# Holding GpSimd's work until the VectorE op ahead of the planner's last two-port VectorE op has ended

## The chip, the cores and the metric

The kernel runs on one NeuronCore of one Trainium2 chip. The metric is device time in microseconds (us), from the first to the last instruction of one execution, with medians over several executions. Every execution counted here is classed "fast" unless I say otherwise; where the granted clock of TensorE (PE) was below 1.0 in an execution, I say so too, since with one core the class alone does not show it.

## The reference

One pre-norm transformer layer on x of 2048 x 512 in bfloat16: attention with 32 heads of 16, then a gated feed-forward part of width 1792.

```python
h  = x + softmax(q @ k.T * 16**-0.5) @ v @ wo        # q, k, v from layernorm(x) @ wqkv, 32 heads
h2 = h + (gelu(ln(h) @ w_gate) * (ln(h) @ w_up)) @ w_down
```

The costly part is the exponential of 32 x 2048 x 2048 scores: the exponentials on ScalarE alone keep it busy for 724.1 of the 812.7 us of the profiled execution of before.

## The kernel before

The kernel holds a planner. It describes all work as operations with an engine, an estimated length, tiles that are read and written, and priorities; it plays them through on its own clock, and whenever an operation is started there, it is emitted into the instruction stream of its engine. The chip then runs these fixed streams. Besides its place in the stream and the conflict that `port` stands for (below), what holds an instruction back on the chip are semaphores, and these come from the data: a read waits for the write, a write for earlier reads.

```python
class Op:
    def __init__(self, eng, dur, fns, reads=(), writes=(), ..., port=False, ...):
        ...
        self.port = port or eng == "pool"

class Sched:
    def _ready(self, op):                    # earliest planned start
        ...
        return max([self.done[t] + LATS.get((t[0], op.eng), LAT) + lag for t in toks ...]
                   + [self.port if op.port else 0.0])

    def _emit(self, op, start):
        ...
        extra = op.extra() if op.extra else ()
        for tok in extra:
            start = max(start, self.done[tok] + LATS.get((tok[0], op.eng), LAT))
        ...
        end = start + op.dur
        if op.port:
            self.port = end
        # ... cut: transfers, PE groups
        for i, fn in enumerate(op.fns):
            tok = P.op(op.eng, fn, reads=op.reads, writes=op.writes, sig=(i == n - 1), extra_deps=extra)
```

`port` stands in the plan for a conflict between VectorE and GpSimd. All GpSimd ops ("pool") and some VectorE ops ("dve") take it, and in the plan they take it one after the other. A VectorE op with `port=True` is called two-port below, the products included; "two-port", "port" and "queue" are names for what the rows of the trace show, and no more is claimed. In 44 rows, 20.7 us in all, a two-port VectorE op takes longer than usual, 1.79 us in place of 0.94 for instance (L1730 at 458.56 us, shown in the prediction). Each of the 44 overlaps a GpSimd op that began earlier and ends 0.54 to 0.55 us (L1728, L1735) or 0.80 to 0.82 us (L1730) after it. Where no GpSimd row overlaps, no row of these lines is longer than 0.70, 0.70 and 0.96 us. The other way round, the GpSimd product L1732 takes 1.15 us in 88 rows and about 1.53 in 35; these 35 begin while a two-port VectorE op runs and end 1.01 to 1.02 us after it. So the one that came first holds the other up. VectorE's L1715, which reads PSUM and is not two-port, shows nothing of the kind: 54 of its 492 rows lie wholly under a GpSimd row, and none is longer than 0.69 us. The chip does not keep the order of the plan: 43 of the 44 are blocked by a GpSimd op that was emitted after them.

Exponentials are made in two ways. ScalarE takes most (778 instructions, L1347). For the rest, in groups of four tiles, VectorE makes an exponential from bit patterns (the `pbank` tiles lie in PSUM, where PE's products land; the `dXE` tiles lie in SBUF; lines are shortened here, cuts are marked by dots):

```python
    def dconv(G, j, b):      # four times for each group, from PSUM, not marked `port` (L1715)
        yield Op("dve", 0.603, lambda e: e.tensor_scalar(out=dXE[...][:, 0, j, :], in0=pbank[:, b, :], ...), ...)

    def dchain(G):           # n = 4 tiles of 512, nd = 3 of them for VectorE
        yield Op("dve", 0.07 + 0.133 * n, lambda e: e.tensor_scalar(out=W, in0=X, ...), ..., port=True)          # L1728
        yield Op("dve", 0.066 + 0.267 * nd, lambda e: e.tensor_tensor(out=W[:, 0:nd, :], ..., op=ALU.mult),
                 ..., port=True)                                                                                  # L1730
        for j in range(nd, n):
            yield Op("pool", TPOOL, lambda e, j=j: e.tensor_tensor(out=W[:, j, :], ..., op=ALU.mult),
                     reads=[kW[j], kX[j], kW[0]], writes=[kW[j]], port=True)                                      # L1732
        yield Op("dve", ..., lambda e, ...: e.tensor_scalar(out=X, in0=X, ...), reads=kX + kW, ..., port=True)    # L1735
        sch.add(group_pv(G), -5.1)     # PE multiplies both halves with V
```

There are 123 such groups. GpSimd also masks Q (L1533), scales attention outputs (L1841) and makes the layer norm's statistics (L1426, L1428, L1910, L1911).

## Time and profile before

| | before |
|---|---|
| median | 814.82 us (814.54 to 814.97, 3 runs) |
| busy: PE, ScalarE, VectorE, GpSimd | 97%, 95%, 93%, 30% |
| chain that ended last | PE 49%, VectorE 30%, ScalarE 10% |

In the profile's rows "L1730 DVE ..." is line 1730 of the kernel on VectorE, then output and input tiles, the count, the busy time in us and the mean of one in ns, and after the bar the idle time ahead of these instructions with what ended most of it. A row of waits reads: who, for whom, us in total, times, longest. A row of the timeline reads: start, length, engine, line, what, and in brackets an idle time before it. The rows of before stand in the prediction.

### The profile page before, as it was taken

To read this page: it belongs to the slowest core of one execution; us is meant where nothing else is said; L and a number is where in the kernel's file an instruction comes from. 1 tells how busy PE (TensorE), PEld (TensorE's weight loads), DVE (VectorE), ACT (ScalarE), POOL (GpSimd) and SP (SyncE) were. 2 spreads that over 40 slices of the span, in tenths; PEclk is the share of its full clock that TensorE was granted. 3 is DMA by queue.
4 is the path that set the end of the run, shared out by engine and by line. 5 is a ranking of instruction groups with operands and counts; after the bars stand their busy time and mean duration, and the time that the engine had idled before them with its cause. 6 is when DMAs were issued, how large, how long until landed. Compare 5 with 4: busy or idle time off the path is not lost.

```text
span 812.7 us, 20343 instructions
## 1 busy us (share of the span) xinstructions
PE 792.2 (97%) x8342; PEld 276.0 (34%) x8342; DVE 758.9 (93%) x1236; ACT 769.8 (95%) x815; POOL 246.6 (30%) x283
## 2 busy tenths in 40 slices
PE   8999999999999999999999999999999999999998
PEld 4222222222222222222233333333443343444557
DVE  8679999999999999999999999999999999999965
ACT  5899999999999999999999999999999999999972
POOL 3513345532343222122143232223224222233210
PEclk9999999999999999999999999999999999999999
DMA  6200000610021000010011000010001100110000
GB/s 208 52 8 1 7 8 7 252 48 8 7 53 28 8 7 1 8 28 21 23 46 30 11 9 21 14 28 27 8 21 28 27 8 8 28 29 16 15 22 19
DMA packets 50022, 24.33 MB, mean 30 GB/s; under 512 B 39296, under 2 KB 48896, under 8 KB 49920
## 3 DMA queue, kind: packets, MB, share of 16 engines
q1 hardware_dynamic: 49776, 22.88, 10.8%
q8 instruction: 67, 1.10, 0.5%
q14 instruction: 35, 0.29, 0.1%
q10 hardware_dynamic: 144, 0.07, 0.0%
HBM read 11.80 MB, written 2.10 MB: 17 GB/s over the span
## 4 chain that ended last, share of the span: by engine, by line
PE 49%; DVE 30%; ACT 10%; issue 5%; POOL 2%; DMA 0%; DVEq 0%; ACTq 0%; POOLq 0%
PE pbank L1341 31%; PE pbank L1340 14%; DVE dXE L1715 12%; ACT PT L1347 8%; DVE dXE L1730 5%; DVE dXE L1728 4%; PE pbank L2090 4%; DVE dXE L1735 4%; DVE GUT L1981 1%; POOL dXE L1732 1%; ACT GUT L1994 1%; DVE OA L1819 1%; DMA xnT<-xn_sb 0%; ACT L1347 0%; POOL xn_sb L1442 0%
## 5 line engine op out<-in xcount | busy, mean ns | idle before, releaser
L1347 ACT ACTIVATE PT<-pbank 128x1024 bf16<-128x1024 f32 x778 | 724.1, 1080 | 13.4 <-PE pbank L1341 10.2
L1341 PE MATMUL pbank<-QT,KT 32*128 32x512 bf16 (+1 forms) x2304 | 346.9, 359 | 8.4 <-DVE dXE L1715 3.3
L1715 DVE TENSOR_SCALAR dXE<-pbank 128x512 uint16<-128x512 f32 x492 | 323.0, 680 | 8.8 <-PE pbank L1341 6.7
L1732 POOL TENSOR_TENSOR dXE<-dXE 128x512 f16<-128x512 f16 x123 | 155.3, 1263 | 369.2 <-DVE dXE L1730 369.2
L1341 PEld LDWEIGHTS pbank<-QT,KT 32*128 32x128 bf16 x2304 | 89.2, 91 | 294.3 <-ACT PT L1347 201.9
L1341 PE MATMUL pbank<-PT,VA 128*32 128x256 bf16 (+2 forms) x2708 | 130.1, 292 | 0.0
L1730 DVE TENSOR_TENSOR dXE<-dXE 128x1536 f16<-128x1536 f16 x123 | 122.1, 993 | 1.1
L1728 DVE TENSOR_SCALAR dXE<-dXE 128x2048 uint16<-128x2048 uint16 x123 | 94.3, 767 | 0.1
L1735 DVE TENSOR_SCALAR dXE<-dXE 128x2048 uint16<-128x2048 uint16 x123 | 88.1, 720 | 5.8 <-POOL dXE L1732 4.8
L1341 PE MATMUL pbank<-dXE,VA 128*32 128x256 f16 (+2 forms) x1752 | 76.2, 289 | 2.0 <-DVE dXE L1735 1.9
L1340 PE MATMUL pbank<-hnT_c,wg_sb 128*128 128x256 bf16 (+2 forms) x392 | 70.4, 291 | 0.0
L1341 PEld LDWEIGHTS pbank<-PT,VA 128*32 128x32 bf16 x2708 | 47.4, 96 | 60.3 <-issue 57.1
L2090 PE MATMUL pbank<-ones_bf,zero_bf 128*128 128x512 bf16 x201 | 66.0, 386 | 0.0
L1340 PE MATMUL pbank<-hnT_c,wu_sb 128*128 128x256 bf16 (+2 forms) x392 | 58.0, 289 | 3.9 <-DVE GUT L2009 3.2
L1340 PE MATMUL pbank<-wd_sb,GUT 128*128 128x512 bf16 (+1 forms) x238 | 59.9, 369 | 0.0
L1841 POOL TENSOR_TENSOR Otok<-OAT,LINV 128x128 bf16<-128x128 bf16 (+2 forms) x52 | 30.1, 593 | 80.5 <-DVE LINV L1835 79.9
L1341 PEld LDWEIGHTS pbank<-dXE,VA 128*32 128x32 bf16 x1752 | 31.0, 96 | 32.2 <-issue 17.2
L1340 PE MATMUL pbank<-xnT,wqkv_sb 128*128 128x512 bf16 (+1 forms) x152 | 38.2, 349 | 0.9 <-DMA xnT<-xn_sb 0.8
L2009 DVE TENSOR_TENSOR GUT<-pbank,GUT 128x512 bf16<-128x512 f32 (+1 forms) x57 | 36.6, 670 | 1.9 <-PE pbank L1340 1.3
L1340 PEld LDWEIGHTS pbank<-hnT_c,wu_sb 128*128 128x128 bf16 x392 | 29.7, 98 | 24.1 <-issue 9.1
L1981 DVE CAST GUT<-pbank 128x512 bf16<-128x512 f32 (+1 forms) x53 | 35.4, 672 | 1.4 <-PE pbank L1340 1.3
L1533 POOL TENSOR_SCALAR QT<-QT,qmask 128x512 bf16<-128x512 bf16 x30 | 26.3, 883 | 32.7 <-DVE QT L1530 31.8
(82 smaller groups left out, 344.1 us busy)
## 6 DMA issues: line engine op xcount, KB each, us to landing
xres<-in_A_x_dram SPq DMA_DIRECT2D x16, 128.0 KB, 2.2
out_dram<-out_sb SPq DMA_DIRECT2D x15, 128.0 KB, 1.7
wg_sb<-in_B_w_gate_dram SPq DMA_DIRECT2D x1, 1792.0 KB, 7.1
wu_sb<-in_B_w_up_dram SPq DMA_DIRECT2D x1, 1792.0 KB, 11.1
wd_sb<-in_B_w_down_dram SPq DMA_DIRECT2D x1, 1792.0 KB, 15.3
x_sb<-in_A_x_dram SPq DMA_DIRECT2D x3, 512.0 KB, 9.2
wqkv_sb<-in_A_wqkv_dram SPq DMA_DIRECT2D x1, 896.0 KB, 8.5
x_sb<-in_A_x_dram SPq DMA_DIRECT2D x2, 256.0 KB, 2.9
```

What stands on the lines that cost most here:

```text
L1340: return lambda e: e.matmul(o, l, r, start=start, stop=stop)
L1341: return lambda e: e.matmul(o, l, r, start=start, stop=stop, tile_position=tile)
L1347: return lambda e: e.activation(out=o, in_=i, func=func, **kw)
L1715: yield Op("dve", 0.603, lambda e: e.tensor_scalar(out=dXE[G["k"] % NX][:, 0, j, :], in0=pbank[:, b, :], scalar1=XMIN + 1024.0 * CENTER, s ...
L1728: yield Op("dve", 0.07 + 0.133 * n, lambda e: e.tensor_scalar(out=W, in0=X, scalar1=0x3ff, scalar2=0xb800, op0=ALU.bitwise_and, op1=ALU.bi ...
L1730: yield Op("dve", 0.066 + 0.267 * nd, lambda e: e.tensor_tensor(out=W[:, 0:nd, :].bitcast(F16), in0=W[:, 0:nd, :].bitcast(F16), in1=X[:, 0 ...
L1732: yield Op("pool", TPOOL, lambda e, j=j: e.tensor_tensor(out=W[:, j, :].bitcast(F16), in0=W[:, j, :].bitcast(F16), in1=X[:, j, :].bitcast( ...
L1735: yield Op("dve", 0.07 + 0.133 * (h1 - h0), lambda e, h0=h0, h1=h1: e.tensor_scalar(out=X[:, h0:h1, :], in0=X[:, h0:h1, :], scalar1=0x7c00 ...
L1841: yield Op("pool" if turned else "dve", 0.15 + 0.55 / len(slots) if turned else 0.06 + 0.28 / len(slots), lambda e, o4=o4, lx=lx, o_ap=o_a ...
L1981: yield Op("dve", 0.07 + 0.001042 * n * CHUNKS[c], lambda e: e.tensor_copy(out=o_ap, in_=i_ap), reads=[("pb", b)], writes=keys, extra=dE)
L2009: yield Op("dve", 0.07 + 0.001042 * n * CHUNKS[c], lambda e: e.tensor_tensor(out=o_ap, in0=u_ap, in1=o_ap, op=ALU.mult), reads=[("pb", b)] ...
L2090: return Op("pe", TMM, lambda e: e.matmul(pbank[:, b, :], zero_bf[:], ones_bf[:], start=False, stop=False, skip_group_check=True), reads=[ ...
```

## The change

The intent is to make the chip follow the plan where VectorE and GpSimd hold each other up. Let X be the last two-port VectorE op emitted before a GpSimd op. Each GpSimd op now depends, besides on its data, on the VectorE op that stands just ahead of X. So GpSimd is meant not to take the port ahead of X, and yet to stand ready when X ends. Where the new wait ends later than the waits that were there, I call the GpSimd op held.

```diff
         self.port = 0.0
+        self.port_tok = self.dve_tok = None
@@ _emit
         extra = op.extra() if op.extra else ()
+        if op.eng == "pool" and self.port_tok:
+            extra = list(extra) + [self.port_tok]
@@ after the instruction is placed
+            if op.eng == "dve":
+                if op.port:
+                    self.port_tok = self.dve_tok
+                self.dve_tok = tok
```

## The prediction

20.3 - 8, about 12 us, x 0.55 is 6.6 us, two thirds of it were taken as 4.5, and 814.8 - 4.5 is 810.3 us. "Lock", here and in the expectations, is what I call the port.

> **What bounds the kernel now.** I read the page first, then the waits, then the chain of work that ended last, then the timeline of VectorE and GpSimd side by side. There is one core at full clock throughout, so no state and no die is in question. The totals by stretch (columns: stretch, its length, then busy time and instruction count of PE, weight loads, VectorE, ScalarE, GpSimd, then clock, DMA share, GB/s) show three engines that are full at once:
>
> ```profile
> 40.00:780.00 740.00, 726.63 (x7624) 240.25 (x7623) 714.72 (x1125) 730.22 (x768) 226.41 (x235) 1.00 0.10 25
> ```
>
> In these 740 us ScalarE lacks 9.8 us, PE 13.4 us, VectorE 25.3 us. VectorE's work can become shorter by any amount; as long as the 778 exponentials stay on ScalarE, the steady stage cannot give back much more than what ScalarE and PE lose there. The waits say what they lose:
>
> ```profile
> ACT PT L1347 <- PE pbank L1341: 10.2, 21, 1.7
> PE pbank L1341 <- DVE dXE L1715: 3.3, 9, 0.7
> PE pbank L1341 <- DVE dXE L1735: 1.9, 6, 0.7
> DVE dXE L1735 <- POOL dXE L1732: 4.8, 6, 1.3
> ```
>
> ScalarE waits for score products of PE (10.2 us in 21 waits), and PE in turn for VectorE. The chain puts VectorE on 30% of the span. Now the three VectorE lines of the "other exponential" chain (mask, product, mask) and GpSimd's fourth of that product, in the page's groups:
>
> ```profile
> L1732 POOL TENSOR_TENSOR dXE<-dXE 128x512 f16<-128x512 f16 x123 | 155.3, 1263 | 369.2 <-DVE dXE L1730 369.2
> L1730 DVE TENSOR_TENSOR dXE<-dXE 128x1536 f16<-128x1536 f16 x123 | 122.1, 993 | 1.1
> L1728 DVE TENSOR_SCALAR dXE<-dXE 128x2048 uint16<-128x2048 uint16 x123 | 94.3, 767 | 0.1
> L1735 DVE TENSOR_SCALAR dXE<-dXE 128x2048 uint16<-128x2048 uint16 x123 | 88.1, 720 | 5.8 <-POOL dXE L1732 4.8
> ```
>
> L1728 and L1735 are the same operation on the same size, yet they average 767 and 720 ns. The timeline shows why: nearly all take 0.68 us, and a few much more. One case, VectorE's rows first, then GpSimd's:
>
> ```profile
> 456.98 0.95 DVE L1730 TENSOR_TENSOR dXE<-dXE 128x1536 f16<-128x1536 f16 x1
> 457.84 0.69 DVE L1728 TENSOR_SCALAR dXE<-dXE 128x2048 uint16<-128x2048 uint16 x1
> 458.56 1.79 DVE L1730 TENSOR_TENSOR dXE<-dXE 128x1536 f16<-128x1536 f16 x1
> 460.27 0.68 DVE L1715 TENSOR_SCALAR dXE<-pbank 128x512 uint16<-128x512 f32 x1
> ```
>
> ```profile
> 458.00 1.54 POOL L1732 TENSOR_TENSOR dXE<-dXE 128x512 f16<-128x512 f16 x1 [6.43 <-DVE dXE L1730]
> ```
>
> ```profile
> 461.01 0.60 PE L1341 MATMUL pbank<-QT,KT 32*128 32x512 bf16 x3 [0.70 <-DVE dXE L1715]
> ```
>
> GpSimd is released 0.07 us after the first L1730 ends, loses to L1728, which has just begun, and takes 1.54 us in place of 1.15. Then the second L1730 loses to GpSimd: 1.79 us in place of 0.94, that is 0.85 us blocked, until 459.54 when GpSimd ends. PE then stands still for 0.70 us and ScalarE for 0.61 us.
>
> [...] of 492 L1715 (from PSUM), 480 last 650 to 699 ns and none longer, with GpSimd busy or not. [...] here L1732 falls cleanly into 88 of 1.15 us and 35 of about 1.53, so I use 1.15.
>
> **The change part by part.** It computes nothing more and removes nothing: it adds a wait to GpSimd's stream. In the planner every GpSimd op and the listed VectorE ops occupy one "port" in turn, so a GpSimd op is emitted with a planned start after the end of the last two-port VectorE op (call it X) emitted before it. The chip knows nothing of this plan: GpSimd starts when its data are there. Now it also waits for the VectorE op in front of X. As the planned start is already after the end of X, the new dependency cannot move a planned start: X lasts at least 0.327 us in the plan, and the token of its predecessor counts as seen 0.083 + 0.12 = 0.203 us after that predecessor's end. So I expect the same instructions in the same order on every engine, and only waits to differ.
>
> Step 1, how many waits. The profile has no emission order across engines, so I listed the order in which the kernel before emits its VectorE and GpSimd ops (an order, no times) and laid it against the trace; all 1236 and 279 ops match by line. For 94 GpSimd ops the predecessor of X is later than anything that they already wait for. For 82 of these it ended no earlier than 0.05 us before the recorded start, so there the wait is real: 35 of L1732, 25 of L1841, 12 of L1533, 6 of L1910, 3 of L1911, 1 of L1426. The delay to the predecessor's end is 76 us in sum, 38 of it on L1732 (1.1 us each).
>
> Step 2, what VectorE gets back. Every two-port op above its usual length (678 ns for L1728 and L1735, 941 for L1730, 400 for L1912) by 40 ns or more: 44 ops, 20.7 us. For 43 of them (20.3 us) the blocking GpSimd op is emitted after the blocked op: precisely what the wait forbids, since VectorE goes from X's predecessor to X within about 0.03 us, or even 0.08 us before its recorded end, while GpSimd's start follows the end by 0.07 to 0.09. So X wins. By line: 10.6 us of L1728, 5.6 of L1730, 4.1 of L1735.
>
> Step 3, what it pays. [...] GpSimd now runs after X, and L1735 of that group must wait for it. From X's end GpSimd needs 1.15 us plus some 0.15 of two releases, 1.3 us; the VectorE ops between X and that L1735 cover 0.6 us each. By position of L1735 after X: directly in 4 of the 35 (1.3 us idle each), second in 5 (0.7), third in 15 (0.1), later in 11 (nothing): 5.2 + 3.5 + 1.5 = 10.2 us. Some 2 us of this VectorE waits today already (part of its 4.8 us), so net 8. Net for VectorE: 20.3 - 8 = about 12 us.
>
> Step 4, what reaches the end. Of the 20.7 us blocked, 11.4 lie on the chain, when each op's excess is weighted by its part on it: 55%. So 12 x 0.55 = 6.6 us on the path that ends last. PE and ScalarE follow close behind and the PE stream holds its filler products in fixed places (L2090, 201 of them), so I keep two thirds: 4.5 us. 814.8 - 4.5 = **810.3 us**, 0.55% faster.
>
> **The rivals.** (a) Only moved: in bursts of port work the sum of port time is what counts and it makes no difference who goes first. From 405.6 to 412.7 us three groups run through one after another, and VectorE has nothing but two-port work; 2.66 us of blocked time lie there, and I work out by hand that reordering returns 0.4. None of it is on the chain. If all cases were so: 814 to 815. Against it: in most of the 35 cases two or more PSUM reads (L1715), which need no lock, follow X. (b) A wait takes the place: GpSimd is in order, so a held L1841 or L1533 holds an L1732 behind it, and L1735, and 33 weight loads of PE already wait for L1735, 11.5 us in all. That could give 816 to 819. Against it: GpSimd is 30% busy, and the plan that ordered everything has these waits inside. (c) All the blocked time on the chain comes back and no new wait does: 814.8 - 11.4 = 803.4. Against it: it would take most of what ScalarE lacks (9.8 us). (d) A late GpSimd delays the statistics or the output scaling (L1910, L1841: 24.5 us of added delay in sum) and so a transpose that PE waits for. Nothing waits for them in the list of PE's waits today.
>
> **Range and chances.** Centre 810.3. The low end, 804.5, is (c) nearly in full; the high end, 815.0, is (a). Faster by over 2% means under 798.5 us, 16.3 us gained, more than ScalarE lacks in the whole steady stage: 2%. Slower by over 2% needs 831: 1%. Within 2%: 97%. The runs of before lie within 0.43 us, so half a per cent will show.
>
> **What the profile after would show.** Step 1: the same instruction counts on every engine (8342, 1236, 815, 283). Step 2: the mean of L1728 falls from 767 to about 690 ns, L1730 from 993 to 950, L1735 from 720 to 690; hardly a row of 1.26 or 1.79 us is left; VectorE's busy time falls by about 20 us. GpSimd's own rows get longer, because they are now released just as X takes the lock: mean of L1732 from 1263 to about 1400 ns, GpSimd's busy time from 247 to about 285. Step 3: "L1735 waits for L1732" rises from 4.8 us to about 12, in more than 20 places. Step 4: "ScalarE waits for L1341" falls from 10.2 to about 7. I am wrong if L1728 keeps its rows of 1.26 us (then X does not win the lock), if the L1735 wait grows by 20 us (rival b), or if VectorE loses 20 us and the time does not move (then VectorE was not on the path, and the chain misled me).

## The result, and the profile after

| | before | after |
|---|---|---|
| median | 814.56 us (814.17 to 814.97, 6 runs) | 809.08 us (808.80 to 809.29, 6 runs) |
| mean length of L1728, L1730, L1735 | 767, 993, 720 ns | 683, 950, 722 ns |
| blocked time of two-port VectorE ops | 20.7 us in 44 ops | 4.6 us in 6 ops |
| VectorE waits at L1735 for the product L1732 | 4.8 us, 6 times | 10.9 us, 15 times |
| VectorE busy | 758.9 us | 745.8 us |
| last exponential of ScalarE ends at | 786.4 us | 780.7 us |

The ratio is 0.9933 (95% interval 0.9920 to 0.9945). The gain of 0.7% is far above the spread of the runs. A ratio is the mean time of one kernel's fast runs over that of the other's of the same rounds, so it is not quite the ratio of the medians. "Blocked time", here and below, is worked out from the single rows of the trace as in the prediction: the excess of each two-port op over its usual length, where it is 40 ns or more. The changed kernel has seven lines more in that part, so L1728, L1730, L1732, L1735, L1341 and L1347 of before are L1735, L1737, L1739, L1742, L1348 and L1354 of after (and of most of the experiments). In the text I keep the numbers of before, in the profile rows they are those of the kernel shown.

A listing of both programs shows the same instructions in the same order on all five engines. Only semaphore values differ.

The groups of after that answer to the four rows of before:

```profile
L1739 POOL TENSOR_TENSOR dXE<-dXE 128x512 f16<-128x512 f16 x123 | 166.1, 1353 | 327.4 <-DVE dXE L1737 241.3
...
L1737 DVE TENSOR_TENSOR dXE<-dXE 128x1536 f16<-128x1536 f16 x123 | 116.8, 950 | 1.1
L1742 DVE TENSOR_SCALAR dXE<-dXE 128x2048 uint16<-128x2048 uint16 x123 | 88.4, 722 | 11.7 <-POOL dXE L1739 10.9
L1735 DVE TENSOR_SCALAR dXE<-dXE 128x2048 uint16<-128x2048 uint16 x123 | 84.0, 683 | 0.1
```

L1728 and L1730 are at their usual length on average: none is blocked any more. L1735 is not: its mean did not move. GpSimd's product takes longer by its rows (1353 ns, was 1263), as they include time spent in the queue for the port: in e3_wait_for_x below, where it never queues, the mean is 1153 ns.

The case shown in the prediction, in the timeline of after, VectorE first, then GpSimd:

```profile
455.55 0.95 DVE L1737 TENSOR_TENSOR dXE<-dXE 128x1536 f16<-128x1536 f16 x1
456.42 0.69 DVE L1735 TENSOR_SCALAR dXE<-dXE 128x2048 uint16<-128x2048 uint16 x1
457.14 0.96 DVE L1737 TENSOR_TENSOR dXE<-dXE 128x1536 f16<-128x1536 f16 x1
458.01 0.68 DVE L1722 TENSOR_SCALAR dXE<-pbank 128x512 uint16<-128x512 f32 x1
458.61 0.68 DVE L1988 CAST GUT<-pbank 128x512 bf16<-128x512 f32 x1
459.21 0.68 DVE L1742 TENSOR_SCALAR dXE<-dXE 128x2048 uint16<-128x2048 uint16 x1
```

```profile
457.18 1.92 POOL L1739 TENSOR_TENSOR dXE<-dXE 128x512 f16<-128x512 f16 x1 [6.24 <-DVE dXE L1735]
```

GpSimd's product is now released by L1728 (here L1735: the first mask of the next group, the op ahead of X), 0.07 us after its end and 0.04 us after X has begun. X, the second product, takes 0.96 us where it took 1.79. GpSimd's row lasts 1.92 us in place of 1.15: it stands in the queue for the rest of X and is done at 459.10, 1.00 us after X's recorded end. Meanwhile VectorE does two ops that read PSUM, and GpSimd's work is hidden under them. PE had stood still for 0.70 us here; in after no wait of PE or ScalarE falls between 452 and 463 us.

The waits of after, ScalarE, PE and VectorE:

```profile
ACT PT L1354 <- PE pbank L1348: 8.0, 13, 1.7
...
PE pbank L1348 <- ACT PT L1354: 6.9, 25, 0.5
...
PE pbank L1348 <- DVE dXE L1722: 1.0, 2, 0.7
...
DVE dXE L1742 <- POOL dXE L1739: 10.9, 15, 1.6
...
DVE dXE L1722 <- PE pbank L1348: 8.1, 25, 1.1
```

ScalarE waits for scores less and PE for VectorE's L1715 far less (3.3 us in 9 before). What takes their place are waits in the other direction: PE for ScalarE, 6.9 us in 25 (before: 1.1 us in 5), and VectorE for PE, 8.1 us in 25 (before: 6.7 in 19). VectorE runs ahead, and the tight engines are now PE and ScalarE. The wait of L1735 for GpSimd's product has more than doubled. The chain that ended last says the same:

```profile
PE 67%; ACT 14%; DVE 11%; issue 6%; POOL 1%; DMA 0%; ACTq 0%; POOLq 0%
```

VectorE had 30% of it and has 11%. The stretch from 40 to 780 us (PE, weight loads, VectorE, ScalarE, GpSimd):

```profile
40.00:780.00 740.00, 716.68 (x7713) 243.21 (x7786) 702.29 (x1126) 733.52 (x774) 244.05 (x235) 1.00 0.10 25
```

ScalarE lacks 6.5 us there in place of 9.8, VectorE 37.7 in place of 25.3. (PE's busy time is not to be compared here: the profile of after lacks 80 matmul records that the program has, 8262 of 8342.)

One place where the change buys little is the burst of three groups around 405 us of before. In the timelines of VectorE and GpSimd in after:

```profile
403.06 0.95 DVE L1737 TENSOR_TENSOR dXE<-dXE 128x1536 f16<-128x1536 f16 x1
403.92 0.69 DVE L1735 TENSOR_SCALAR dXE<-dXE 128x2048 uint16<-128x2048 uint16 x1
404.64 0.96 DVE L1737 TENSOR_TENSOR dXE<-dXE 128x1536 f16<-128x1536 f16 x1
405.52 0.69 DVE L1735 TENSOR_SCALAR dXE<-dXE 128x2048 uint16<-128x2048 uint16 x1
406.24 0.96 DVE L1737 TENSOR_TENSOR dXE<-dXE 128x1536 f16<-128x1536 f16 x1
408.24 2.23 DVE L1742 TENSOR_SCALAR dXE<-dXE 128x2048 uint16<-128x2048 uint16 x2 [1.04 <-POOL dXE L1739]
```

```profile
406.28 3.03 POOL L1739 TENSOR_TENSOR dXE<-dXE 128x512 f16<-128x512 f16 x2 [3.27 <-DVE dXE L1735]
```

All products of VectorE run unhindered, and then GpSimd's two held products run one behind the other. VectorE waits 1.04 us for the first, and of its next two L1735 one is blocked by the second (2.23 us for both; unhindered it would be 1.28). From the start of the first product to the end of the third L1735 it was 9.89 us before (404.70 to 414.59) and is 9.33 us now (403.06 to 412.39).

What blocks the L1735 here is the same in four of the six blocked ops of after (0.95 us each, 3.8 of the 4.6 us): VectorE waits in L1735 for a held product, GpSimd goes straight on to the next held product, and that one takes the port 0.07 us before L1735 starts. In three of the four the blocked L1735 is the X of the op that blocks it, so X did not win there. The wait for the op ahead of X protects X only where VectorE goes on to X at once, and here X itself waits for GpSimd.

### The profile page after: what moved, and what is told of

Its sections match the earlier page's. It is cut to its first block, busy times and chain, and to the rows that moved or that the text cites. A ratio compares the mean times of both kernels' runs of the same rounds, so it can differ in the third digit from the quotient of the medians.

```text
span 807.1 us, 20270 instructions
## 1 busy us (share of the span) xinstructions
PE 776.0 (96%) x8262; PEld 275.5 (34%) x8342; DVE 745.8 (92%) x1236; ACT 767.5 (95%) x815; POOL 263.7 (33%) x283
## 3 DMA queue, kind: packets, MB, share of 16 engines
q8 instruction: 66, 1.08, 0.6%
## 4 chain that ended last, share of the span: by engine, by line
PE 67%; ACT 14%; DVE 11%; issue 6%; POOL 1%; DMA 0%; ACTq 0%; POOLq 0%
PE pbank L1348 43%; PE pbank L1347 21%; ACT PT L1354 12%; DVE dXE L1722 4%; PE pbank L2097 2%; DVE dXE L1737 2%; DVE dXE L1742 2%; ACT GUT L2001 1%; DVE dXE L1735 1%; ACT L1354 1%; POOL dXE L1739 1%; DMA xnT<-xn_sb 0%; DVE stats L1423 0%; DVE OA L1826 0%; PE pbank L2093 0%
## 5 line engine op out<-in xcount | busy, mean ns | idle before, releaser
L1354 ACT ACTIVATE PT<-pbank 128x1024 bf16<-128x1024 f32 x778 | 721.7, 1095 | 10.0 <-PE pbank L1348 8.0
L1348 PE MATMUL pbank<-QT,KT 32*128 32x512 bf16 (+1 forms) x2304 | 343.6, 359 | 11.2 <-ACT PT L1354 6.9
L1739 POOL TENSOR_TENSOR dXE<-dXE 128x512 f16<-128x512 f16 x123 | 166.1, 1353 | 327.4 <-DVE dXE L1737 241.3
L1348 PEld LDWEIGHTS pbank<-QT,KT 32*128 32x128 bf16 x2304 | 88.8, 91 | 290.6 <-ACT PT L1354 213.5
L1348 PE MATMUL pbank<-PT,VA 128*32 128x256 bf16 (+2 forms) x2708 | 130.1, 292 | 0.0
L1737 DVE TENSOR_TENSOR dXE<-dXE 128x1536 f16<-128x1536 f16 x123 | 116.8, 950 | 1.1
L1742 DVE TENSOR_SCALAR dXE<-dXE 128x2048 uint16<-128x2048 uint16 x123 | 88.4, 722 | 11.7 <-POOL dXE L1739 10.9
L1735 DVE TENSOR_SCALAR dXE<-dXE 128x2048 uint16<-128x2048 uint16 x123 | 84.0, 683 | 0.1
L1348 PE MATMUL pbank<-dXE,VA 128*32 128x256 f16 (+2 forms) x1752 | 76.2, 289 | 1.8 <-DVE dXE L1742 1.8
L1347 PE MATMUL pbank<-hnT_c,wg_sb 128*128 128x256 bf16 (+2 forms) x392 | 70.4, 291 | 0.0
L1348 PEld LDWEIGHTS pbank<-PT,VA 128*32 128x32 bf16 x2708 | 47.4, 96 | 60.6 <-issue 57.4
L1848 POOL TENSOR_TENSOR Otok<-OAT,LINV 128x128 bf16<-128x128 bf16 (+2 forms) x52 | 34.3, 668 | 93.2 <-DVE LINV L1842 41.7
L1347 PE MATMUL pbank<-hnT_c,wu_sb 128*128 128x256 bf16 (+2 forms) x392 | 58.0, 289 | 3.4 <-DVE GUT L2016 2.7
L1347 PE MATMUL pbank<-wd_sb,GUT 128*128 128x512 bf16 (+1 forms) x212 | 54.2, 367 | 4.0 <-issue 3.8
L2097 PE MATMUL pbank<-ones_bf,zero_bf 128*128 128x512 bf16 x163 | 54.5, 385 | 2.7 <-issue 2.7
L1348 PEld LDWEIGHTS pbank<-dXE,VA 128*32 128x32 bf16 x1752 | 30.9, 96 | 31.6 <-issue 18.1
L1540 POOL TENSOR_SCALAR QT<-QT,qmask 128x512 bf16<-128x512 bf16 x30 | 28.0, 938 | 37.6 <-DVE QT L1537 25.0
L1347 PE MATMUL pbank<-xnT,wqkv_sb 128*128 128x512 bf16 (+1 forms) x152 | 38.2, 349 | 1.1 <-DMA xnT<-xn_sb 0.8
L1347 PEld LDWEIGHTS pbank<-hnT_c,wu_sb 128*128 128x128 bf16 x392 | 29.8, 98 | 23.3 <-issue 8.9
```

Source lines behind the costliest of these rows:

```text
L1347: return lambda e: e.matmul(o, l, r, start=start, stop=stop)
L1348: return lambda e: e.matmul(o, l, r, start=start, stop=stop, tile_position=tile)
L1354: return lambda e: e.activation(out=o, in_=i, func=func, **kw)
L1742: yield Op("dve", 0.07 + 0.133 * (h1 - h0), lambda e, h0=h0, h1=h1: e.tensor_scalar(out=X[:, h0:h1, :], in0=X[:, h0:h1, :], scalar1=0x7c00 ...
L1848: yield Op("pool" if turned else "dve", 0.15 + 0.55 / len(slots) if turned else 0.06 + 0.28 / len(slots), lambda e, o4=o4, lx=lx, o_ap=o_a ...
L2097: return Op("pe", TMM, lambda e: e.matmul(pbank[:, b, :], zero_bf[:], ones_bf[:], start=False, stop=False, skip_group_check=True), reads=[ ...
```

## The experiments

Ten kernels ran, each beside runs of before on the same chip. Five differ from before only in semaphore values: the listing shows its instructions and order on every engine. Three change the size of an instruction and keep the order, and two have a new plan. All gave correct results except the two that are wrong on purpose.

My theory: X now wins the port, which gives back what the product in front of it used to block. The rivals: the gain comes from the other GpSimd work; any later start of GpSimd would do; GpSimd's readiness in the queue matters and not only who is first; the wait itself costs something that hides part of the gain.

### e1_product_only: the wait on the product alone

```diff
-        if op.eng == "pool" and self.port_tok:
+        if op.eng == "pool" and self.port_tok and op.writes[0][0] == "dE":
```

> The new wait on GpSimd's fourth of the product (L1732 of before) alone; the plan and the order on every engine are kept. Theory (the two-port VectorE op X now wins the lock): of the 20.3 us of blocked time that the wait forbids, 18.2 us come from this product, so about 0.9 of the 5.5 us gained: 809.3 to 810.0 us, blocked time of the two-port VectorE ops down to about 7 us (4.6 that the changed kernel keeps and 2.1 from the other GpSimd ops). Rival 1 (the gain comes from GpSimd's other work being moved out of the way): near 814. Rival 2 (holding the output scaling and the masks costs something, that the changed kernel pays): under 808.5.

Measured: 809.34 us (809.09 to 809.56, 5 runs) against 814.64, ratio 0.9934. Blocked time 6.7 us. The gain is the product's, all of it within the noise.

### e2_all_but_product: the wait on everything else

```diff
-        if op.eng == "pool" and self.port_tok:
+        if op.eng == "pool" and self.port_tok and op.writes[0][0] != "dE":
```

> The new wait on all GpSimd work except the product. Theory: only 2.1 us of blocked time come from these ops, half of it on the path: 813.5 to 814.6 us, and blocked time of about 18 us stays. Rival 1 (the other GpSimd work is what mattered): 810 to 812. Rival 2 (its delay costs): over 815.

Measured: 814.94 us (814.28 to 815.17, 5 runs), ratio 0.9999 (0.9987 to 1.0012); blocked time 17.3 us. This is the same as before: neither the small gain that I expected nor a cost. Blocked time fell by 3.4 us, and the wait of L1735 for the product rose from 4.8 to 6.8 us. In the groups of this run L1728 (here L1735) stays long:

```profile
L1735 DVE TENSOR_SCALAR dXE<-dXE 128x2048 uint16<-128x2048 uint16 x123 | 93.0, 756 | 0.1
```

The first rival falls with these two runs.

### e3_wait_for_x: released at the end of X

The planned starts are kept; only the token in the instruction stream is another.

```diff
                 if op.port:
-                    self.port_tok = self.dve_tok
+                    self.port_tok = tok
                 self.dve_tok = tok
```

> GpSimd waits for X itself, the last two-port VectorE op in front of it in the plan, not for the op ahead of X. X wins the lock as in the changed kernel, but GpSimd now starts one release (0.08 us) after X's end in place of taking over the lock at once. Theory: blocked time as low as in the changed kernel (about 4.6 us); GpSimd's rows shorter (the product's mean falls from 1353 to about 1200 ns, as it no longer stands in the lock's queue); VectorE's wait for the product grows from 10.9 to 12 to 15 us; time 809.1 to 810.5. Rival (what counts is that GpSimd stands ready in the queue when X ends): over 811.

Measured: five executions at full clock took 811.46 to 812.20 us; a sixth took 818.08 at a clock of 0.987. The median of all six is 811.98, the ratio with the sixth in it 0.998. So it gains about half of what the changed kernel gains, and the rival's bound (over 811) is met, not mine. Blocked time is even lower (2.8 us), so X wins here as well; what is lost lies in the hand-over:

```profile
L1739 POOL TENSOR_TENSOR dXE<-dXE 128x512 f16<-128x512 f16 x123 | 141.7, 1153 | 351.1 <-DVE dXE L1737 204.6
...
L1742 DVE TENSOR_SCALAR dXE<-dXE 128x2048 uint16<-128x2048 uint16 x123 | 86.0, 702 | 20.2 <-POOL dXE L1739 16.2
```

GpSimd never queues any more (1153 ns), but VectorE waits 16.2 us for it in place of 10.9. Laid against the emission order, the 35 products that the change holds end 1.01 us after X's recorded end in the changed kernel and 1.23 us after it here (medians; quartiles within 0.004 us of them). 35 x 0.222 = 7.8 us that GpSimd is later, of which 2.9 us (811.98 - 809.08) reach the end. Who is first matters, and so does that the second stands in the queue when the first ends. As an estimate from these numbers, the queued product works as if it had started 0.14 us (1.15 - 1.01) ahead of X's recorded end.

### e4_two_ahead: released one op too early

```diff
                 if op.port:
-                    self.port_tok = self.dve_tok
+                    self.port_tok = self.dve_tok2
+                self.dve_tok2 = self.dve_tok
                 self.dve_tok = tok
```

> GpSimd waits for the VectorE op two ahead of X, one op too early. The number of waits is much the same, GpSimd is still held back, but it is released while the op ahead of X runs and takes the lock before X where that op needs no lock. Theory (who wins the lock is all): by the trace of before only 5.2 of the 20.7 us blocked are protected, 15.5 us stay; time 812.5 to 814.0. Rival (any later start of GpSimd, or merely a stream closer to the plan, gives the gain): 809 to 811.

Measured: 819.01 and 819.46 us in the two executions at full clock, 827.5 to 831.1 in the four with a mean clock of 0.98 to 0.99. I had expected a small gain and got a loss, even at full clock. Blocked time rose to 25.4 us, and 24.0 us of it lies on the X ops (15.8 us before). The profiled execution is one of those with the lowered clock (831.07 us), but the next run shows the same blocked time at 0.998. My count had only asked which of the old conflicts the wait would remove. It had not asked which it would make: held until the op two ahead of X has ended, GpSimd starts while the op ahead of X runs and takes the port just in front of X. "Any later start will do" is refuted: a later start at the wrong place is worse than none (at full clock this rests on two executions).

### e9_two_ahead_product: the same on the product alone

> The wait for the op two ahead of X again, on the product alone, and on a fresh set of executions. The first such kernel was slower than before (819.0 to 819.5 us at full clock, four of six executions longer with a granted clock of 0.98 to 0.99), against what I had expected. Explanation to test: GpSimd, released while the op ahead of X runs, takes the lock just before X, so that more X are blocked than before. If so: 816 to 820 us at full clock, blocked X over 18 us. If it was the other GpSimd ops, or the chip's clock alone: 812 to 815 at full clock. And if the lowered clock belongs to this kernel's way of running, it shows again in several executions; if it was that chip's hour, it does not.

Its edit is that of e4_two_ahead with the condition of e1_product_only. Measured: 819.99 us (clock 0.998) to 832.67 (clock 0.979), median 826.2; blocked time 25.2 us, of it 23.4 on X. The loss is the product's, and it came back. The timelines of VectorE and GpSimd in this run, where L1730, L1735 and L1732 are L1738, L1743 and L1740, at the end of a bad stretch:

```profile
270.01 1.79 DVE L1738 TENSOR_TENSOR dXE<-dXE 128x1536 f16<-128x1536 f16 x1
...
272.32 1.26 DVE L1743 TENSOR_SCALAR dXE<-dXE 128x2048 uint16<-128x2048 uint16 x1
273.50 1.28 DVE L1723 TENSOR_SCALAR dXE<-pbank 128x512 uint16<-128x512 f32 x2
```

```profile
269.45 1.53 POOL L1740 TENSOR_TENSOR dXE<-dXE 128x512 f16<-128x512 f16 x1 [2.69 <-DVE dXE L1743]
271.88 1.16 POOL L1740 TENSOR_TENSOR dXE<-dXE 128x512 f16<-128x512 f16 x1 [0.90 <-DVE dXE L1738]
```

Two VectorE ops are blocked in a row, by 0.85 and 0.58 us, and PE pays (timeline of PE, same run):

```profile
274.84 0.38 PE L1349 MATMUL pbank<-QT,KT 32*128 32x512 bf16 x1 [1.14 <-DVE dXE L1723]
```

PE stands still for 1.14 us, and from 276.08 us on the record of the clock shows half speed for 3.41 us. In the profiled run of e4_two_ahead the same place has a gap of 1.13 us that ends at 275.05, and half speed from 275.27 us for 30.72 us. The stretches of that run, with the clock in the last column but two:

```profile
250.00:270.00 20.00, 19.45 (x149) 4.86 (x149) 19.59 (x34) 20.00 (x23) 5.20 (x8) 1.00 0.13 27
270.00:310.00 40.00, 38.87 (x205) 6.74 (x203) 28.94 (x42) 28.58 (x30) 8.17 (x8) 0.62 0.02 4
310.00:330.00 20.00, 20.00 (x154) 4.97 (x153) 18.35 (x31) 19.93 (x22) 3.87 (x4) 1.00 0.04 8
```

So in both traces the half clock begins within 1.3 us after the end of such a gap. The traces of before and after show no PE gap of 1 us near that place and no half clock within the work (the record of the clock begins at 5.3 us): it first stands there at 814.2 and 807.3 us, after the last instruction (812.7 and 807.1). That the gap brings the half clock about is not shown: other gaps, 1.39 us at 492 us of before and 1.79 us at 784 us of e4_two_ahead itself, bring none. What brings it about stays open. The lowered clock does not belong to these two kernels alone either: of the 39 executions of before, one took 821.85 us at 0.989 and one 816.30 us at 0.998, and one of the six of e3_wait_for_x ran at 0.987. None of these was profiled.

### e5_before_tiny and e6_after_tiny: GpSimd's product cut to two columns

The lines are shortened.

```diff
-  e.tensor_tensor(out=W[:, j, :].bitcast(F16), in0=W[:, j, :].bitcast(F16), in1=X[:, j, :].bitcast(F16), op=ALU.mult)
+  e.tensor_tensor(out=W[:, j, 0:2].bitcast(F16), in0=W[:, j, 0:2].bitcast(F16), in1=X[:, j, 0:2].bitcast(F16), op=ALU.mult)
```

Both give a wrong result on purpose (relative error 0.55), and a range check on the row sums is widened so that the same path runs.

> The kernel before with GpSimd's product cut from 512 to 2 columns (a wrong result on purpose; the range check of the row sums is widened so that the path stays the same; the plan and the order are kept). It takes away nearly all of the lock conflict and all waits for the product, so it shows what the conflict costs in all. Theory: blocked time under 3 us (the masks and the output scaling stay), no wait of L1735 for GpSimd; 803 to 807 us. Rival (the path has room, PE and ScalarE hold the end at about where the changed kernel is): 808 to 809.5.

Measured: 807.05 us (806.70 to 807.41, 6 runs); blocked time 2.6 us, the wait of L1735 for GpSimd 0.5 us. This is about the floor of this plan as far as the product on GpSimd goes: the conflict over the port and the waits for the product together cost 814.60 - 807.05 = 7.6 us, and the change recovered 5.5 of them. It lies 0.05 us above the range of "803 to 807" that I expected.

> The same cut in the changed kernel: against the previous run it shows what the added waits cost by themselves, with nothing to gain from them. Theory (a wait on an engine that is 33% busy is free): within 1 us of the previous run. Rival (the wait itself delays the end of the chain): 2 us or more slower than the previous run.

Measured: 806.47 us (806.25 to 806.76, 6 runs), 0.6 us faster than the run without the waits. The waits cost nothing that can be seen; the small gain fits the blocked time, 2.6 us without and 0.07 us with them, but that reason is argued and not shown by itself.

### Three attempts at a better version

`TPOOL = 1.11` became `TPOOL = 1.25` on the changed kernel:

> An attempt at a better version: the changed kernel with the planner told that the product takes 1.25 us in place of 1.11, so that it leaves more VectorE work between X and the op that waits for GpSimd. The plan changes. If the 10.9 us of waiting for GpSimd matter: that wait halves, 806 to 808.5 us. If a changed plan costs as much elsewhere, or the waits are off the path: 808.5 to 813.

Measured: 817.47 us (815.60 to 818.83), ratio 1.0028; the one execution at full clock took 815.60, the others ran at 0.996 to 0.998. The wait for GpSimd fell to 6.4 us as hoped, but the new plan has 120 groups in place of 123, so ScalarE does 784 exponentials in place of 778. At 0.917 us each, the median spacing of the ends of two exponentials in the trace of before, that is 5.5 us more, most of the 6.5 us between the full-clock execution and the changed kernel's 809.08.

VectorE takes the whole product when three groups are in the chain at once (the line that counts `gfull` is left out):

```diff
         C["gw"] += 1
+        if C["gfull"] - C["gdone"] >= 3:      # groups converted and not yet done
+            nd = n
```

> A second attempt: where three groups are in the chain at once (bursts in which VectorE has nothing but lock-taking work, so that GpSimd's share hides under nothing), VectorE takes the whole product. The plan changes. If bursts cost what the trace suggests (a wait of 1 us and a blocked op of 0.96 us in each): 806 to 808.5 us; the wait for GpSimd falls to under 7 us. If the changed plan gives it back: 808.5 to 813.

Measured: 811.56 us (810.50 to 812.87), ratio 0.9954. The wait for GpSimd fell to 5.0 us with the same 815 ScalarE instructions, yet 2.5 us were lost against the changed kernel. Where they went in the new plan I did not settle. VectorE multiplies all four tiles in 31 of the 123 groups, 1218 ns in place of 951, about 8.3 us more work. ScalarE now waits 10.0 us for the last gates, which it did for 2.2 us, but 5.8 us less for the output and 3.3 us less for the gates from VectorE.

The product split otherwise, plan and order kept (in outline, not the lines themselves):

```diff
-  VectorE: W[:, 0:3, :]  (1536 columns)     GpSimd: W[:, 3, :]     (512)
+  VectorE: first 1664 columns               GpSimd: W[:, 3, 128:]  (384)
```

> An attempt at a better version with the plan and the order kept: the changed kernel with a quarter of GpSimd's columns (128 of 512) given to VectorE's product, 1664 columns in place of 1536. VectorE's product gets longer by about 0.07 us (8 us in all), GpSimd's shorter by about 0.25 us. The floor without GpSimd's product was 807 us. If the waits for GpSimd are what is left: wait of L1735 for GpSimd under 6 us and 807.5 to 809. If VectorE's longer product costs the same: 809 to 810.5, no better than the changed kernel.

Measured: 809.18 us (808.69 to 809.60, 5 runs), ratio 0.9934. The rows of the product on VectorE and of the op behind it:

```profile
L1739 DVE TENSOR_TENSOR dXE<-dXE 128x1664 f16<-128x1664 f16 x123 | 125.1, 1017 | 1.1
L1744 DVE TENSOR_SCALAR dXE<-dXE 128x2048 uint16<-128x2048 uint16 x123 | 86.9, 710 | 7.3 <-POOL dXE L1741 7.3
```

VectorE waits 3.6 us less and works 8.3 us more (125.1 - 116.8). The time is that of the changed kernel. None of the three beats it.

## Why the prediction was right or wrong

The prediction (810.3 us, range 804.5 to 815.0) was right: 809.08 us. Its steps one by one.

**The order stays.** Right: the program listings are equal on all engines. The promised count of 8342 matmul records did not show, since 80 records are missing in the profile of after; the program has them.

**Step 2, what VectorE gets back.** Right for L1728 and L1730: predicted about 690 and 950 ns, measured 683 and 950, and not one of them blocked. Wrong for L1735: predicted 690, measured 722. The step asked which conflicts the wait forbids and took all other pairs as unchanged. The six blocked ops that remain, 4.6 us, are all L1735: four behind a pair of held products, as shown above, two (0.8 us) behind other GpSimd work. Three of them are an X that lost, against "So X wins": the step had VectorE go from X's predecessor to X within 0.03 us, and that fails where X waits for the product ahead. VectorE's busy time therefore fell by 13.1 us and not by about 20. The same one-sided count misled me in e4_two_ahead.

**Step 3, what it pays.** The wait of L1735 for GpSimd was to rise to about 12 us in more than 20 places: 10.9 us in 15. The total is near, its two terms are not. The step had L1735 wait 1.3, 0.7 or 0.1 us when it is first, second or third after X. In after, three of the four in first place wait about 1.08 us, four of the five in second about 0.45 and one of the 15 in third: 5.9 us in eight places, not 10.2. In e3_wait_for_x the medians are 1.34, 0.67 and 0.07 us: the step had reckoned the hand-over by a release at X's end, and GpSimd that stands in the queue is quicker (done 1.01 us after X, not 1.23). And the 2 us that were to be among the waits of before were not: all six of before (4.8 us) lie behind products that are not held, and such waits are still there (4.9 us in seven). So the rise is 6.1 us for a predicted net of 8; the two errors cancel in part, which is luck. Net for VectorE: 20.7 - 4.6 blocked less 6.1 more waiting is 10.0 us; predicted 12.

**Step 4, what reaches the end.** 55% on the chain, then two thirds for the engines close behind, 4.5 us in all. Measured 5.5 of 10.0 us: 55%, without the further cut. So the two-thirds term was too cautious at this size and the 12 us too large, and the two cancel in part. That 55% came out is itself partly luck, since the share is no constant: in e1_product_only 8.9 us of VectorE time gave 5.3, in e3_wait_for_x 6.5 gave 2.7. The cut does become real further on. With nearly all of the conflict gone (e5_before_tiny), 18.1 us less blocked time and 4.3 us less waiting gave 7.6 us: the last 2.1 us of gain cost 12.4 us of VectorE time (18.1 + 4.3 - 10.0). That fits the bound drawn from the 9.8 and 13.4 us that ScalarE and PE lack; that they set the pace there is argued, not shown by itself.

**GpSimd's own time.** Predicted 285 us and 1400 ns for the product, measured 263.7 and 1353. Of the product's rise of 11 us, predicted 17, all is on the 35 held ones. I had counted the queueing of every held op as new; but 9 of the 35 stood in the queue before, too, and 6 do not now. For GpSimd's other work I had some 21 us more and 6 came; that I did not take apart.

**The rivals.** (a), only moved, holds in bursts: I had put 0.4 us on the one around 405 us, and 9.89 - 9.33 = 0.56 us came. (b), a wait in the place of the blocked time, is present as 6.1 us and smaller than what it replaces; in e6_after_tiny the waits by themselves cost nothing that can be seen. (c), everything back and no new wait, would have been 803.4; the measured floors are 807.05 and, with the waits, 806.47. (d), late statistics or scaling: e2_all_but_product holds just these and shows no cost.

ScalarE's wait for scores was to fall from 10.2 to about 7 us and fell to 8.0.

## What to carry to other kernels

Where two engines hold each other up as here (1.79 us for a VectorE product in place of 0.94, 1.53 for GpSimd's in place of 1.15), compare the mean of a group of equal ops with its usual single row: the excess is blocked time, and the rows of the other engine tell who blocked. The remedy can be a dependency on the op *ahead* of the one that should win: the loser stands in the queue and was done 1.01 us after the winner's end here, against 1.23 us when it was released at that end. The wait for the op ahead gave 809.1 us; one op later lost half of the gain (812.0), one op earlier turned it into a loss (819.0 to 819.5 at full clock, before 814.6). It fails where the winner itself still waits for the loser's engine (three of the six blocked ops of after). When counting what a new wait will give, count the conflicts that it creates as well as those that it removes.
